# The first batch's x loads, the copies of the filter's first step and the conversion of the weights, rearranged

## The chip, the cores and the metric

The kernel runs on one core of a Trainium2 chip. The metric is the device time of one execution in microseconds (us). Five engines work side by side, each in the order of its own instructions, and wait for each other by semaphores: PE (TensorE, matmuls), DVE (VectorE), ACT (ScalarE), POOL (GpSimd), and SP (SyncE), which issues the DMAs here.

## What is computed

Two blocks in a row. The first filters x with a long convolution, the second is a gated layer on the result:

```python
h = relu(pos_emb @ w1) @ w2 * exp(-0.01 * arange(S))[:, None]      # the filter, S = 12480
y = irfft(rfft(x * v, n=2*S, axis=1) * rfft(h, n=2*S, axis=0), n=2*S, axis=1)[:, :S]
a = (x * y).reshape(4 * S, 128)                                    # 4 batches, 128 channels
t = a @ moe_w_in                                                   # 128 x 2048, float64 words
out = (t * cos(t)) @ moe_w_out                                     # 2048 x 128, float64 words
```

## The kernel before

The convolution is done by transforms of length 96 x 120, written as matmuls against tables of sines, in four steps: a first forward step (f1, matmuls of L449), a second one with the product by the filter's spectrum (f2), and two inverse steps (i1, i2). The filter and the first batch go through f1 and f2 before all else; the other three batches' transforms run beside the gated layer, which makes up most of the time. This change is wholly in the beginning, up to the end of the first batch's f1.

Program order there is laid down by hand with Python generators: a loop runs through the yields of one and calls `next` on others in between, so what is emitted at which yield fixes the order on every engine. Engines run their own instructions in that order.

- **u, the product x * v of the first batch.** `u_units` (L598) cuts it into 30 slices. For each, `u_load` loads x and v (`load_pairs`, L404), three slices ahead; `u_multiply` (L429) multiplies the two halves in place in x's tile (L431: from slice 8 on, the first half on POOL, the second on DVE), and `u_sums` (L433) writes the sum and the difference of the halves into `slots` (L441: the sum on POOL in odd slices from 9 on, all else on DVE). x and v have five buffers each, both in unused room of the big tile `slots` (class `Between`, L292), in rows of 128 elements that lie apart. So each slice takes four DMAs with runs of 512 bytes: two halves of x and two of v.
- **The filter's rows** (`filter_out`, L387, matmuls L391, copies L397 by ACT) are made from 25 to 52 us, with 52 steps of u between them.
- **f1** (`f1_units`, L625) goes through 64 channel pairs, first of the filter, then of the batch. A pair has one PSUM bank of eight, filled by four matmuls (two yields to a pair; the trace has eight rows of PE for a pair). Then it is copied out: for the filter in two copies (`f1_evict_filter`, L468 and L470), for the batch in one (`f1_evict`, L461). `taker` (L453) chooses ACT or DVE by a share: 0.8 of the filter's pairs go to ACT, which leaves DVE every fifth, and 0.75 of the batch's.
- **Conversions.** moe_w_in and moe_w_out come as float64. `convert_units` (L176) loads them as pairs of 32-bit words in 16 pieces of 256 KB (`raw`, three buffers; the first six are issued on ACT's queue, the rest by SP), makes float32 of them with integer operations, and stores them to DRAM (L190). A piece goes through all engines but PE: `float32_begin` (L142) is DVE L147 and L149, POOL L151, ACT L154 and L155, POOL L156; `float32_end` (L159) is DVE L160 and L162, POOL L166. `float32_end` of a piece is emitted just before `float32_begin` of the next.
- **The joining loop** (after L958) runs through f1's yields, numbered i. At three of four it takes a step of u, until those are done; at i = 40 it starts the conversions' first two loads, and from i = 63 on, at every ninth i, it takes a conversion step. So the first conversion stands, on every engine, right behind the last steps of u.
- **Table stores.** `store_tables` (L282) has ACT L284 and six DMAs by SP (L285 to L288), emitted before f1, that is ahead of the loads of the last nine slices of u.
- **f2** (`f2_both_units`, L653): makes its weights w with ACT L322 and DVE L324 and multiplies with L482, L485 and L135. Its first w is made when the conversions are over; its pool lies where that of the conversions was.

Of the kernel before, what the change touches and what calls it, by code (L numbers as in the profile page):

```python
# [10 lines left out]
F32 = mybir.dt.float32  # L11
# [3 lines left out]
ALU = mybir.AluOpType  # L15
# [19 lines left out]
def kernel(  # L35
# [46 lines left out]
    nc = tc.nc  # L82

    B, S, D = x.shape
# [3 lines left out]
    R = S // N2  # L88
# [8 lines left out]
    FR = 2 * (2 * N2 - 2 * N1)  # L97
    KF = N1 - 2 * (N2 - N1)
    CB = D // 2
# [5 lines left out]
    UA = 2  # L105
# [3 lines left out]
    assert G == 2 * UA and H % UA == 0 and N2 % G == 0  # L109
    LAG = 7  # L110
    ALONE = 8
    WCOL = 256

    dram = ctx.enter_context(tc.tile_pool(name="dram", bufs=1, space=DRAM))
# [24 lines left out]
        nc.tensor.transpose(dst, src, ident[0:n, 0:n])  # L139


    def float32_begin(pool, raw, factor):  # L142
        lo, hi = raw[:, :, 0], raw[:, :, 1]

        power = pool.tile([P, WCOL], U32, name="power", bufs=3)
        sig = pool.tile([P, WCOL], U32, name="sig", bufs=2)
        nc.vector.tensor_scalar(out=power[:, :], in0=hi, scalar1=20, scalar2=0x7FF,  # L147
                                op0=ALU.logical_shift_right, op1=ALU.bitwise_and)
        nc.vector.tensor_scalar(out=sig[:, :], in0=hi, scalar1=0xFFFFF, scalar2=0x100000,  # L149
                                op0=ALU.bitwise_and, op1=ALU.bitwise_or)  # L150
        nc.gpsimd.tensor_scalar(out=power[:, :], in0=power[:, :], scalar1=1023.0 - 127.0,  # L151
                                scalar2=0.0, op0=ALU.subtract, op1=ALU.max)
        high, low = sig[:, :].bitcast(F32), lo.bitcast(F32)
        nc.scalar.activation(high, sig[:, :], AF.Copy, scale=factor * 2.0 ** -20)  # L154
        nc.scalar.activation(low, lo, AF.Copy, scale=factor * 2.0 ** -52)  # L155
        nc.gpsimd.tensor_tensor(high, high, low, op=ALU.add)  # L156
        return power, hi, high

    def float32_end(power, hi, high):  # L159
        nc.vector.tensor_scalar(out=power[:, :], in0=power[:, :], scalar1=255.0,  # L160
                                scalar2=float(1 << 23), op0=ALU.min, op1=ALU.mult)
        nc.vector.scalar_tensor_tensor(  # L162
            out=power[:, :], in0=hi, scalar=0x80000000, in1=power[:, :],
            op0=ALU.bitwise_and, op1=ALU.bitwise_or)
        there = power[:, :].bitcast(F32)
        nc.gpsimd.tensor_tensor(there, high, there, op=ALU.mult)  # L166
        return there

    in_words = moe_w_in.bitcast(U32).rearrange("d (f w) -> d f w", w=2)
# [1 line left out]
    pieces = [(wind[:, c:c + WCOL], in_words[:, c:c + WCOL, :], INV_TWO_PI)  # L171
              for c in range(0, DFF, WCOL)]
# [255 lines left out]

    def u_multiply(tiles, half, engine):  # L429
        xt, vt = (t[:, half] for t in tiles)  # L430
        engine.tensor_tensor(xt, xt, vt, op=ALU.mult)  # L431

    def u_sums(u, tiles, a, takers):  # L433
# [191 lines left out]
    def f1_units(bank, u, share, evict=f1_evict):  # L625
        def mm(j, ps, i):
            if i == 0:
                ps = bank()
            f1_mm(ps, u, j, i)
            return ps  # L630

        return units(CB, F1_STEPS, lambda j: None, mm, lambda j, ps: evict(ps, j, share), 2)

    def f2_units(bank):
        with tc.tile_pool(name="there", bufs=3) as pool:
# [126 lines left out]
    def forward_units(bank, back):  # L762

        f2 = f2_units(bank)
        next(f2)
        yield from f1_units(bank, slots[0:R, :, :, :], 1.0)
        yield from f2
        next(back)
        yield from i1_units(bank)
# [114 lines left out]
    with tc.manual_schedule():  # L884
        with tc.tile_pool(name="psum", bufs=8, space=PSUM) as psum, \
                ExitStack() as first:
            def bank():
                return psum.tile([P, BANK], F32, name="ps")
# [10 lines left out]
            with tc.tile_pool(name="layers", bufs=1, side="right") as pool:  # L899
                w1_sb = pool.tile([P, P], F32, name="w1_sb")  # L900
                nc.gpsimd.memset(w1_sb[:, :], 0.0)
                pes = {0: filter_load(pool, 0)}
                for m in range(2):
                    nc.sync.dma_start(
                        w1_sb[m * FO:(m + 1) * FO, m * FO:(m + 1) * FO], w1[:, :])
                for i in range(1, NCH):
                    pes[i] = filter_load(pool, i)
                    if i == 3:
                        for m in range(2):
                            for n in range(2):  # L910
# [5 lines left out]
                first_u = u_units(0, slots[0:R, :, :, :],  # L916
                                  lambda j, half: nc.vector if half or j < ALONE else nc.gpsimd,
                                  lambda j, i: xvs[i][j % 5], 3,
                                  lambda j: (nc.gpsimd if j >= ALONE and j % 2
                                             else nc.vector, nc.vector))  # L920
# [24 lines left out]
                nc.scalar.activation(c1[:, 2, :], c1[:, 0, :], AF.Copy, scale=-1.0)  # L945
# [4 lines left out]
            for j in range(H // 2):  # L950
                filter_out(bank, aT, ftile, j, w2_sb)
                if j and j % 3 == 0:
                    last_sines.finish()
                for _ in range(2 if j % 2 or j > 15 else 1):
                    next(first_u)
            store_tables()
            keep.__exit__(None, None, None)

            backs = [inverse_units(lambda: bank(), b) for b in range(B)]

            f1 = chain(f1_units(bank, ftile[0:FR, :, :, :], 0.8, f1_evict_filter),
                       f1_units(bank, slots[0:R, :, :, :], 0.75))
            with tc.tile_pool(name="convert", bufs=1) as pool:
                convert = convert_units(pool)
                for i, _ in enumerate(f1):
                    if i % 4 < 3:
                        next(first_u, None)
                    if i == 40 or i >= 60 and i % 9 == 0:  # L970
                        if next(convert, True):
                            break
            f2 = f2_both_units(bank)
            for i, _ in enumerate(f1):
                if i == 6:
# [71 lines left out]
        for i in range(len(steps) + LAG):  # L1047
# [5 lines left out]
            if i < len(steps):  # L1053
                n, c = steps[i]
# [52 lines left out]
```

## Time and profile before

| | us |
|---|---|
| median of 3 runs | 3686.21 |
| lowest and highest run | 3684.47, 3686.36 |
| the profiled execution | 3683.9 |
| its span, first to last instruction | 3682.1 |
| PE busy in it | 3607.1 |
| DVE, POOL, ACT busy | 2814.1, 2754.7, 2228.2 |
| mean granted clock of PE | 0.997 |
| f1 of filter and batch: first L449 to first L482 | 52.44 to 153.44 |
| last product of u (POOL L441) ends | 86.75 |

All views are of the one profiled execution, and their times count from its first instruction. A row of the timeline gives start, duration, engine, line, operation and tiles, and in brackets how long the engine had stood idle before it and what released it. Matmuls of float32 are pipelined, and two rows follow each matmul instruction here. PEld is PE's weight load. The granted clock is the share of full speed that PE was allowed. The share of DMA is the mean over 16 DMA engines. A wait for several semaphores is put down to the one that came last.

### The profile page before, as it was taken

The numbers are of one execution on the slowest core, as the hardware profiler recorded it, in microseconds if no ns is written. First come the engines' busy times: TensorE is split into PE (matmuls) and PEld (weight loads), VectorE is DVE, ScalarE is ACT, GpSimd is POOL, SyncE is SP. The second block draws the span as 40 slices with busy tenths as digits, with TensorE's granted clock in tenths as the row PEclk, the third lists the DMA queues.
The fourth block names the chain that finished last, engine by engine and source line by source line (L and its number), as shares of the span: only waits on it lengthen the run. The fifth ranks groups of instructions, "written<-read, shape, count | busy, mean of one in ns | idle before, by whom it ended". The sixth has DMA issues, their size and how long they took to land.

```text
span 3682.1 us, 101741 instructions
## 1 busy us (share of the span) xinstructions
PE 3607.1 (98%) x40810; PEld 2550.9 (69%) x40810; DVE 2814.1 (76%) x5295; ACT 2228.2 (61%) x4476; POOL 2754.7 (75%) x3237
## 2 busy tenths in 40 slices
PE   8999999999999999999999999999999999999999
PEld 6777776666668776666677776766667786666666
DVE  7687886688887776688887776578887667777777
ACT  5657666655554556655555556665655446666666
POOL 7666996588874886688874887578884448878877
PEclk9999999999999999999999999999999999999999
DMA  7354540022213550022211552012220350000000
GB/s 187 111 172 126 159 145 29 18 70 70 73 47 87 171 154 29 19 70 70 72 40 36 173 167 73 13 53 70 72 69 16 89 169 22 19 23 20 19 25 14
DMA packets 226318, 281.79 MB, mean 77 GB/s; under 512 B 19168, under 2 KB 163352, under 8 KB 225720
## 3 DMA queue, kind: packets, MB, share of 16 engines
q1 hardware_dynamic: 224984, 273.71, 25.5%
q8 instruction: 324, 5.31, 0.6%
q10 hardware_dynamic: 864, 1.57, 0.1%
q14 instruction: 146, 1.20, 0.1%
HBM read 194.75 MB, written 80.46 MB: 75 GB/s over the span
## 4 chain that ended last, share of the span: by engine, by line
PE 84%; DVE 4%; ACT 1%; POOL 1%; issue 1%; DMA 0%; ACTq 0%; SPq 0%; POOLq 0%; DVEq 0%
PE ph L135 30%; PE cv L135 18%; PE accb L836 17%; PE acca L836 13%; PE cv L449 3%; PE cv L139 1%; DVE gt L811 1%; DVE gt L805 1%; PE ph L139 1%; ACT gt L804 1%; POOL ts L819 0%; ACT tile L867 0%; DVE t L504 0%; POOL ts L822 0%; POOL slots L441 0%
## 5 line engine op out<-in xcount | busy, mean ns | idle before, releaser
L804 ACT ACTIVATE gt<-ph 128x512 int32<-128x512 f32 (+1 forms) x1380 | 823.1, 596 | 1145.0 <-PE ph L135 1087.6
L805 DVE SCALAR_TENSOR_TENSOR gt<-ph,gt 128x512 f32<-128x512 f32 (+1 forms) x1380 | 949.2, 688 | 716.3 <-ACT gt L804 713.6
L819 POOL TENSOR_TENSOR ts<-gt 128x512 f32<-128x512 f32 (+2 forms) x784 | 1005.1, 1282 | 584.8 <-PE accb L836 555.3
L135 PE MATMUL ph<-at,w_in_sb 128*64 128x512 f32 (+1 forms) x5520 | 1427.1, 592 | 13.5 <-ACT tile L867 6.5
L810 ACT ACTIVATE gt<-gt 128x512 f32<-128x512 f32 (+1 forms) x1568 | 971.9, 620 | 4.1 <-DVE gt L805 3.4
L811 DVE TENSOR_TENSOR gt<-ph,gt 128x512 f32<-128x512 f32 (+1 forms) x1380 | 936.9, 679 | 0.0
L836 PE MATMUL accb<-ts,w_out_sb 128*64 128x128 f32 (+2 forms) x9408 | 650.1, 272 | 0.0
L822 POOL TENSOR_TENSOR ts<-ts,gt 128x256 f32<-128x256 f32 (+2 forms) x784 | 574.0, 732 | 61.5
L823 POOL TENSOR_TENSOR ts<-gt,ts 128x256 f32<-128x256 f32 (+2 forms) x784 | 574.0, 732 | 61.5
L836 PEld LDWEIGHTS acca<-gt,w_out_sb 128*64 128x64 f32 x6272 | 398.8, 137 | 267.7 <-issue 231.6
L836 PEld LDWEIGHTS accb<-ts,w_out_sb 128*64 128x64 f32 x9408 | 543.8, 137 | 0.0
L836 PE MATMUL acca<-gt,w_out_sb 128*64 128x128 f32 (+2 forms) x6272 | 479.2, 272 | 0.0
L836 PEld LDWEIGHTS accb<-gt,w_out_sb 128*64 128x64 f32 x3136 | 225.1, 137 | 254.4 <-issue 199.2
L135 PEld LDWEIGHTS ph<-at,w_in_sb 128*64 128x64 f32 x5520 | 353.5, 137 | 33.2 <-ACT tile L867 14.7
L505 POOL TENSOR_TENSOR slots<-slots,t 120x256 f32<-120x256 f32 x383 | 280.2, 738 | 128.6 <-DVE t L504 71.1
L135 PEld LDWEIGHTS cv<-slots,tm 96*64 96x64 f32 (+1 forms) x3840 | 243.3, 126 | 119.9 <-issue 116.0
L836 PE MATMUL accb<-gt,w_out_sb 128*64 128x128 f32 (+1 forms) x3136 | 311.1, 273 | 4.7 <-DVE ot L857 3.1
L836 PE MATMUL acca<-ts,w_out_sb 128*64 128x128 f32 (+1 forms) x3136 | 308.4, 272 | 1.4 <-POOL ts L822 1.3
L135 PE MATMUL cv<-slots,tm 96*64 96x128 f32 (+1 forms) x3840 | 274.5, 285 | 4.1 <-DVE slots L527 3.6
L135 PEld LDWEIGHTS cv<-even,slots 120*64 120x64 f32 (+1 forms) x3072 | 168.3, 125 | 60.7 <-issue 58.7
L836 PEld LDWEIGHTS acca<-ts,w_out_sb 128*64 128x64 f32 x3136 | 201.4, 137 | 2.4 <-POOL ts L822 2.2
L135 PE MATMUL cv<-slots,w 124*64 124x256 f32 (+1 forms) x1152 | 190.4, 405 | 1.9 <-ACT at L793 1.9
(137 smaller groups left out, 3742.4 us busy)
## 6 DMA issues: line engine op xcount, KB each, us to landing
h<-hd SPq DMA_DIRECT2D x144, 240.0 KB
tm<-td SPq DMA_DIRECT2D x96, 312.0 KB
xs<-in_x_dram SPq DMA_DIRECT2D x120, 208.0 KB
zd<-xs SPq DMA_DIRECT2D x119, 208.0 KB
tile<-zd SPq DMA_DIRECT2D x96, 256.0 KB
xt<-in_x_dram SPq DMA_DIRECT2D x90, 208.0 KB
vt<-in_v_dram SPq DMA_DIRECT2D x90, 208.0 KB
w<-wd SPq DMA_DIRECT2D x144, 116.2 KB
```

Of the source, the lines that this page charges most:

```text
L135: nc.tensor.matmul(dst[lo:hi], left[:, lo:hi], right, start=start, stop=stop)
L139: nc.tensor.transpose(dst, src, ident[0:n, 0:n])
L449: nc.tensor.matmul(dst[lo:hi], u[:, b, lo:hi, i], c1[0:u.shape[0], r:r + 2, :].rearrange("p r k -> p (r k)"), start=True, stop=True)
L505: (engine if r else nc.gpsimd).tensor_tensor(y[:, r], y[:, r], t[:, r], op=op)
L804: nc.scalar.activation(turns, ph[:, 0:m], AF.Identity, bias=phase)
L805: nc.vector.scalar_tensor_tensor(out=part, in0=ph[:, 0:m], scalar=phase, in1=turns, op0=ALU.add, op1=ALU.subtract)
L810: nc.scalar.activation(part, part, AF.Sin, scale=scale)
L811: nc.vector.tensor_tensor(part, ph, part, op=ALU.mult)
L819: nc.gpsimd.tensor_tensor(ts[:, 0:2, 0:half], gt[:, :, half:2 * half], gt[:, 0, 0:2 * half].rearrange("p (h n) -> p h n", h=2), op=ALU.sub ...
L822: nc.gpsimd.tensor_tensor(t[2], t[1], b11, op=ALU.add)
L823: nc.gpsimd.tensor_tensor(t[3], b21, t[2], op=ALU.subtract)
L836: nc.tensor.matmul(acc[h * CB:(h + 1) * CB, place, 0:r], w_out_sb[:, pair, weight, :], right[:, h * r:(h + 1) * r], start=(pair == 0 and i ...
```

## The change

It touches the following.

1. The first batch's x gets a pool of its own (`xpool`, five buffers), in tiles whose halves are contiguous, so `load_pairs` makes one DMA of it with runs of 1024 bytes. v stays as it was. The pool is closed when u is done, and that of the conversions is opened where it was.
2. The filter's copies: all pairs up to 36 (XV) go to ACT, the later ones by a share of 0.7; the batch's by 0.7.
3. The joining loop is cut in two: the first runs until u's steps are used up, then the tables are stored, then the second begins with the conversions' loads. Conversion steps come from i = 72 on, at every ninth i and four behind it.
4. A piece is emitted in two parts: `float32_begin` (DVE alone) and, four yields later, `float32_go_on` (POOL and ACT).
5. All raw loads are issued by SP.

```diff
-    def float32_begin(pool, raw, factor):
-        lo, hi = raw[:, :, 0], raw[:, :, 1]
+    def float32_begin(pool, raw):
+        hi = raw[:, :, 1]
...
+        return power, hi, sig
+
+    def float32_go_on(power, sig, lo, factor):
         nc.gpsimd.tensor_scalar(out=power[:, :], in0=power[:, :], scalar1=1023.0 - 127.0,
                                 scalar2=0.0, op0=ALU.subtract, op1=ALU.max)
         high, low = sig[:, :].bitcast(F32), lo.bitcast(F32)
         nc.scalar.activation(high, sig[:, :], AF.Copy, scale=factor * 2.0 ** -20)
         nc.scalar.activation(low, lo, AF.Copy, scale=factor * 2.0 ** -52)
         nc.gpsimd.tensor_tensor(high, high, low, op=ALU.add)
...
-                (nc.scalar if len(raws) < 7 else nc.sync).dma_start(
-                    raws[-1][:, :, :], pieces[len(raws) - 1][1])
+                nc.sync.dma_start(raws[-1][:, :, :], pieces[len(raws) - 1][1])
...
-                begun = float32_begin(pool, raws[i], pieces[i][2])
+                begun = float32_begin(pool, raws[i])
+                yield
+                float32_go_on(begun[0], begun[2], raws[i][:, :, 0], pieces[i][2])
             yield
...
-                xvs = [[between.tile([R, 2 * UA, D], F32).rearrange("p (h n) d -> p h n d", h=2)
-                        for _ in range(5)] for _ in range(2)]
+                vs = [between.tile([R, 2 * UA, D], F32).rearrange("p (h n) d -> p h n d", h=2)
+                      for _ in range(5)]
+                xpool = tc.tile_pool(name="x", bufs=5)
+                xs = xpool.__enter__()
+
+                def first_place(j, i):
+                    if i:
+                        return vs[j % 5]
+                    t = xs.tile([R, 2, UA * D], F32, name="xt")
+                    return t[:, :, :]
...
+            f1 = enumerate(chain(
+                f1_units(bank, ftile[0:FR, :, :, :], lambda b: 0.7 if b > XV else 1.0,
+                         f1_evict_filter),
+                f1_units(bank, slots[0:R, :, :, :], lambda b: 0.7)))
+            for i, _ in f1:
+                if i % 4 < 3 and next(first_u, None) is None:
+                    break
             store_tables()
+            xpool.__exit__(None, None, None)
             keep.__exit__(None, None, None)
...
-            f1 = chain(f1_units(bank, ftile[0:FR, :, :, :], 0.8, f1_evict_filter),
-                       f1_units(bank, slots[0:R, :, :, :], 0.75))
             with tc.tile_pool(name="convert", bufs=1) as pool:
                 convert = convert_units(pool)
-                for i, _ in enumerate(f1):
-                    if i % 4 < 3:
-                        next(first_u, None)
-                    if i == 40 or i >= 60 and i % 9 == 0:
+                next(convert)
+                for i, _ in f1:
+                    if i >= 2 * XV and i % 9 in (0, 4):
                         if next(convert, True):
                             break
```

More of the change, by code (lines that the diff above doesn't have):

```diff
@@ L111 @@
     ALONE = 8
+    XV = 36
     WCOL = 256
@@ L156, in float32_begin, with float32_end @@
         nc.gpsimd.tensor_tensor(high, high, low, op=ALU.add)
-        return power, hi, high
-    def float32_end(power, hi, high):
+    def float32_end(power, hi, sig):
         nc.vector.tensor_scalar(out=power[:, :], in0=power[:, :], scalar1=255.0,
@@ L165, in float32_end @@
         there = power[:, :].bitcast(F32)
-        nc.gpsimd.tensor_tensor(there, high, there, op=ALU.mult)
+        nc.gpsimd.tensor_tensor(there, sig[:, :].bitcast(F32), there, op=ALU.mult)
         return there
@@ L430, in u_multiply @@
         xt, vt = (t[:, half] for t in tiles)
+        if len(vt.shape) > len(xt.shape):
+            xt = xt.rearrange("p (n d) -> p n d", n=UA)
         engine.tensor_tensor(xt, xt, vt, op=ALU.mult)
@@ L630, in mm @@
             return ps
-        return units(CB, F1_STEPS, lambda j: None, mm, lambda j, ps: evict(ps, j, share), 2)
+        return units(CB, F1_STEPS, lambda j: None, mm, lambda j, ps: evict(ps, j, share(j)), 2)
     def f2_units(bank):
@@ L765, in forward_units @@
         next(f2)
-        yield from f1_units(bank, slots[0:R, :, :, :], 1.0)
+        yield from f1_units(bank, slots[0:R, :, :, :], lambda b: 1.0)
         yield from f2
@@ L913 @@
                 between = Between(slots, KE, 2 * N1)
-                xvs = [[between.tile([R, 2 * UA, D], F32).rearrange("p (h n) d -> p h n d", h=2)
-                        for _ in range(5)] for _ in range(2)]
+                vs = [between.tile([R, 2 * UA, D], F32).rearrange("p (h n) d -> p h n d", h=2)
[7 more added lines that the diff above has]
+                    return t[:, :, :]
                 first_u = u_units(0, slots[0:R, :, :, :],
                                   lambda j, half: nc.vector if half or j < ALONE else nc.gpsimd,
-                                  lambda j, i: xvs[i][j % 5], 3,
+                                  first_place, 3,
                                   lambda j: (nc.gpsimd if j >= ALONE and j % 2
@@ L955 @@
                     next(first_u)
+            backs = [inverse_units(lambda: bank(), b) for b in range(B)]
+            f1 = enumerate(chain(
[5 more added lines that the diff above has]
+                    break
             store_tables()
+            xpool.__exit__(None, None, None)
             keep.__exit__(None, None, None)
-            backs = [inverse_units(lambda: bank(), b) for b in range(B)]
-            f1 = chain(f1_units(bank, ftile[0:FR, :, :, :], 0.8, f1_evict_filter),
-                       f1_units(bank, slots[0:R, :, :, :], 0.75))
             with tc.tile_pool(name="convert", bufs=1) as pool:
                 convert = convert_units(pool)
-                for i, _ in enumerate(f1):
-                    if i % 4 < 3:
-                        next(first_u, None)
-                    if i == 40 or i >= 60 and i % 9 == 0:
+                next(convert)
+                for i, _ in f1:
+                    if i >= 2 * XV and i % 9 in (0, 4):
                         if next(convert, True):
                             break
+            f1 = (None for _ in f1)
             f2 = f2_both_units(bank)
```

## The prediction

> **What bounds the kernel now.** I read the page first: PE is busy 98% of the span and its granted clock is full nearly everywhere, so only the few stretches in which PE stands still or runs slowly can give time back. The windows view over the stretches of the first forward step (columns: us, then busy us and instructions of PE, PEld, DVE, ACT, POOL, granted clock, DMA share, GB/s) shows where they are.
> ```profile
> 62.00:84.00 22.00, 15.99 (x183) 14.42 (x179) 12.11 (x29) 7.46 (x28) 11.09 (x14) 0.88 0.78 220
> 84.00:107.00 23.00, 20.25 (x216) 16.63 (x218) 16.16 (x45) 13.89 (x55) 17.07 (x21) 0.82 0.26 87
> 107.00:138.00 31.00, 28.54 (x332) 22.18 (x328) 20.08 (x48) 18.88 (x56) 24.20 (x29) 1.00 0.34 108
> 138.00:154.00 16.00, 15.66 (x187) 13.20 (x188) 5.09 (x10) 10.87 (x27) 2.15 (x3) 1.00 0.09 26
> ```
> PE loses 6 us between 62 and 84, and the clock falls to 0.88 and 0.82. Only the last window runs freely. PE's timeline (start, us, what, idle before) shows the holes:
> ```profile
> 52.44 23.14 PE L449 MATMUL ps<-c,ftile 96*64 96x192 f32 x280 [0.55 <-ACT ftile L397]
> 76.28 0.87 PE L449 MATMUL ps<-c,ftile 96*64 96x192 f32 x8 [0.70 <-DVE slots L470]
> 81.31 1.54 PE L449 MATMUL ps<-c,ftile 96*64 96x192 f32 x8 [4.16 <-DVE slots L470]
> ...
> 138.34 15.17 PE L449 MATMUL ps<-c,slots 104*64 104x192 f32 x184 [0.53 <-ACT slots L461]
> 153.44 0.92 PE L482 MATMUL ps<-ftile,w 124*120 124x256 f32 x3
> ```
> A channel pair is 8 rows; a "slice" below is one of the 30 loads of x and v, a "piece" one of the 16 conversions. 280 rows in 23.14 us are 0.661 us a pair; 184 rows from 138.34 to 153.44 are 0.657. So 128 pairs need about 84.4 us, and the step takes 101.0 (52.44 to 153.44): 16.6 us are lost. The view of waits names the reasons in this stretch:
> ```profile
> ACT sig L154 <- DVE sig L149: 32.3, 16, 14.6
> DVE power L160 <- POOL power L151: 17.9, 16, 1.2
> POOL power L166 <- DVE power L162: 12.1, 16, 0.8
> ```
> ACT stood 14.6 us at the first conversion's L154, with the copies of PE's banks queued behind it, because DVE's L149 lay behind the last products of x and v, which ended at 86.75 (POOL L441). After that the second and third lines are a ring that paces the pieces:
> ```profile
> 111.96 0.83 DVE L160 TENSOR_SCALAR power<-power 128x256 uint32<-128x256 uint32 x1 [1.19 <-POOL power L151]
> 112.82 0.42 DVE L162 SCALAR_TENSOR_TENSOR power<-raw,power 128x256 uint32<-128x256 uint32 x1
> 113.16 0.28 DVE L147 TENSOR_SCALAR power<-raw 128x256 uint32<-128x256 uint32 x1
> ...
> 115.30 0.83 DVE L160 TENSOR_SCALAR power<-power 128x256 uint32<-128x256 uint32 x1 [1.19 <-POOL power L151]
> ```
> One piece takes 3.35 us (111.96 to 115.30): POOL's L166 cannot start before DVE's L162, nor POOL's next L151 before L166, nor DVE's next L160 before L151. PE needs only 4.5 x 0.66 = 2.97 us for the 4.5 pairs that lie between two pieces. So PE, 8 banks ahead at most, is tied to this ring until its end, and the end of the step is: start of piece 0, plus 49.6 us (86.97 to 136.59, the start of piece 15), plus what PE has left after it (136.59 to 153.44, 16.85).
>
> **The change, part by part.**
>
> *The start of piece 0.* Two things count: when the last products end, and when the first raw words are there.
>
> Products: from 41 to 56 DVE and POOL turn in a ring of their own, two slices every 3.62 us (L441 on DVE at 44.35, 47.97, 51.60, 55.22), with no wait on a DMA. Then they slip: a copy pair on DVE (0.45 + 0.25) comes in every fifth channel pair; the six table stores hold SP from 58.57 to 61.72, so the next x load issues at 61.84, some 3.3 us late; and raw loads (three of 256 KB issued on ACT's queue from 65.28 to 74.51) share the DMA engines. The waits on v's DMA on DVE and POOL, 8.8 + 9.4 us in this stretch, follow. The change takes all three away: copies of pairs 0 to 36 are ACT's, stores and raw loads come after the last x and v load. Going on at 3.62 us, DVE's sums of slice 28 start at 55.22 + 6 x 3.62 = 76.94, and POOL's last sum ends about 2.75 later (1.28 + 0.41 + handoffs + 0.97), at 79.7. The gap's memset (0.52) fits into POOL's 1.10 idle of that turn. Against 86.75: 7.0 us.
>
> Do the loads keep up? A slice is 426 KB. With 512-byte runs the trace moved 224 GB/s at a share of 0.78 (41 to 55), SP issuing without pause; I take 0.81 as the most, so some 235 GB/s, 1.81 us a slice, just the ring's pace. Single x or v loads in runs of 1024 show 273 to 293 GB/s at shares of 0.79 to 0.85 (335 to 336 us), so about 280 at 0.81: x then costs 0.76 us instead of 0.905, a slice 1.67. SP issues three DMAs a slice instead of four (0.41 each), 1.4 us instead of 1.8. I take no delay; the far bound is the rate of 224 GB/s kept, 1.90 a slice, over the 14 slices left: 1.3 us. [...] The trace's shares speak for a gain.
>
> Raw words: their pool now lies where x was, so the first load waits for the last sum (its semaphores are those of POOL's and DVE's L441 of slice 29). A new wait of about 2.8 us: the raw load issued at 89.88 moved its data from 90.85 to about 92.0, and the first pe load (issued 0.74, data until 3.3) was taken up at 4.07, so 0.7 from the last data to the taker. From below 2.6, from above 3.3 (pe's whole). Queued behind it are DVE's first copies (pair 40 on), ACT's from pair 37 on, and PE behind these. Piece 0 starts at 79.7 + 0.1 + 2.8 = 82.6 instead of 86.97.
>
> *ACT's copies.* Two per pair take 0.42 us when ACT catches up (88.14, 88.55, 88.97), under PE's 0.66, so taking all of 0 to 36 costs nothing; without that slack each pair would cost its difference. L284 moves into this slack too.
>
> *PE at the join.* ACT stops before pair 37's copy, so PE can finish pair 44: 52.44 + 45 x 0.661 = 82.2. The first copy comes after L149, L154 and L155, about 1.75 us after piece 0 starts (136.59 to 138.34 in piece 15), so PE goes on at 84.35: a hole of 2.1 us in place of 8.8. In the trace the clock fell about 1.5 us into a hole (0.84 in the us from 78) and was half until 92.3, after 5.5 us of work. If it falls, 2.75 us go; but PE then reaches pair 113 at 84.35 + 68 x 0.66 + 2.75 = 132.0, and the ring lets it start that pair only at 134.0. So this is hidden by the ring.
>
> *The parts.* Splitting begin and go-on moves POOL's and DVE's instructions past nothing of their own (their order is the same), so the ring stays 3.35. It moves ACT's L154 and L155 two pairs later and starts the pieces nine half-pairs later in PE's order, so PE is further on when the ring ends. Piece 15 starts at 82.6 + 49.6 = 132.2; ACT frees pair 41 of the second half 1.75 later, so PE starts its pair 49 there (it stood at 41 at this point before). Pair 52 waits for DVE's copy of 46 behind L162: 3.35 + 0.55 + 0.47 + handoff = 4.45 after piece 15. Then the first w (L324) waits for the last store of a converted piece, since its pool lies where the conversions were: POOL's last L166 ends 4.31 after piece 15, its store issues at 4.34 (140.93), its data is through at 142.25, 0.6 more for the receipt: 6.2; two L324 (0.6) and a copy (0.5) bring 7.45, where pair 56 would start at 7.1 otherwise. Eight pairs are left: 7.45 + 8 x 0.657 = 12.7. The receipt could take up to 1 us more (the h store issued at 156.44 is waited for until 160.49).
>
> *Sum.* Step's end: 132.2 + 12.7 = 144.9 instead of 153.44: **8.5 us**, 4.4 by the start of piece 0 and 4.1 by the later place of the pieces. Behind it the order of all engines is the same, PE bound, and shifts as a whole. The profiled execution took 3683.9 (span 3682.1) and so gives 3675.4; it lies 2.3 below the median of the runs, 3686.2, which gives 3677.7. With the bounds (products up to 1.3 later, words 0.2 earlier or 0.5 later, receipt 1 later) 3677.5 to 3680.5.
>
> **Rivals.** *The loads stay behind* (0.22): the loop of five buffers leaves 9.05 us from issue to sums, and one x load now brings both halves at once, so a slice starts only when 208 KB are there. For it: v waits of up to 3.1 us were there with 1.81 us due. Against: they began after SP's late issue. At 2.1 us a slice instead of 1.81 the start slips 4.1: 3681.8; at most 3685.
> *PE's own floor* (0.07): the ring doesn't bind, because ACT's later place lets copies through. The step would end at 52.44 + 84.4 = 136.9, 16.6 gained: 3669.6. Against: DVE's copies still lie between L149 and L160.
> *Slower* (0.05): the five buffers' loop becomes the bound with loads as slow as beside raw words, and the raw words, no longer loaded ahead, add theirs. Each us over 9.05 in the loop costs 14 / 5 = 2.8 us; no gain is left from 3.0 us over (piece 0 at 91.1), and at 5.7 over the time is 3693.7. Against: loads issued at 62.86 landed after 2.8 us (65.64).
> *It doesn't do what it says*: the changed order of instructions has one x DMA a slice and the stores behind the last load, so no chance of its own.
>
> **How the numbers follow.** Forecast 0.66, rivals 0.22, 0.07, 0.05. About 0.2% (7.4 us) can be told from no change, so faster means under 3678.8: three quarters of the forecast's share and the floor's, 0.57; slower means over 3693.6. The range of 3674.5 to 3684.5 leaves out the floor, the slower case and the edge of the second.
>
> **What would show it.** Right: POOL's last sum near 80; the first L147 2.8 us behind it, waiting on the raw words' DMA; PE's hole near 82 to 84; pieces 3.35 us apart; the first L482 near 145. Wrong: waits on v or x before 80, pieces closer or wider than 3.35, a hole between 140 and 145 longer than 1 us, or a later stage that takes the shift back.

## The result, and the profile after

The changed kernel takes 3674.12 us (median of 8 runs, 3673.44 to 3675.01), the kernel before in the same rounds 3686.18 (8 runs, 3683.81 to 3687.70): a ratio of 0.9969, 95% interval 0.9958 to 0.9979 (the two medians alone give 0.9967). It is faster by 12.1 us between the medians; between the two profiled executions by 10.1 (3683.9 and 3673.78) and between their spans by 10.9 (3682.1 and 3671.2). The prediction was 8.5 us: 3675.4 from the profiled execution, 3677.7 from the median. The measured median lies 0.4 us below the lower end of the range that was given (3674.5).

In what follows **the step** is the first forward step, **piece 0** and **piece 15** are the starts of the first and the last conversion (DVE's L148 of each; L147 in the kernel before), and **the rest** is the time from the end of the step to the end of the span. All lines lie a few later in the file: L449 became L455, L441 L447, L154 L158, L160 L163, L166 L169, L468 and L470 became L474 and L476, L461 L467.

The windows view of the changed kernel over the step (us, then busy us and instructions of PE, PEld, DVE, ACT and POOL, then granted clock, DMA share and GB/s):
```profile
62.00:84.00 22.00, 19.18 (x236) 18.81 (x231) 14.18 (x26) 12.82 (x50) 13.51 (x17) 1.00 0.67 188
84.00:107.00 23.00, 22.24 (x236) 18.14 (x238) 16.83 (x46) 14.66 (x56) 17.71 (x22) 0.85 0.34 105
130.00:146.00 16.00, 15.86 (x187) 13.57 (x188) 8.14 (x19) 11.16 (x30) 5.27 (x7) 1.00 0.11 35
```
Between 62 and 84 the trace has 236 rows of PE where it had 183, at a full clock. The clock still falls behind 84 (0.85): a hole is left. PE's timeline shows which (start, us, what, idle before and what ended it):
```profile
51.54 29.65 PE L455 MATMUL ps<-c,ftile 96*64 96x192 f32 x360 [0.55 <-POOL xt L437]
84.76 15.74 PE L455 MATMUL ps<-c,ftile 96*64 96x192 f32 x152 [3.57 <-ACT slots L476]
...
120.11 8.94 PE L455 MATMUL ps<-c,slots 104*64 104x192 f32 x104 [0.44 <-DVE slots L467]
130.14 15.17 PE L455 MATMUL ps<-c,slots 104*64 104x192 f32 x184 [1.09 <-DVE slots L467]
145.24 1.14 PE L488 MATMUL ps<-ftile,w 124*120 124x256 f32 x4
```
One hole of 3.57 us stands where three of 0.70, 4.16 and 3.90 stood. The third of these, in the timeline of the kernel before:
```profile
86.75 20.49 PE L449 MATMUL ps<-c,ftile 96*64 96x192 f32 x216 [3.90 <-DVE slots L470]
```
The step ends at 145.24 instead of 153.44: 8.2 us. The view of waits from 52 to 150 has the ring of the conversions as it was (the second and third lines of this fence are the 16 turns of before). ACT's longest wait at L158 for DVE is 1.8 us instead of 14.6, and the last line is a new wait of 7.0:
```profile
ACT sig L158 <- DVE sig L150: 18.9, 15, 1.8
DVE power L163 <- POOL power L155: 15.4, 16, 1.2
...
POOL power L169 <- DVE power L165: 12.1, 16, 0.8
...
ACT sig L158 <- DMA raw<-in_moe_w_in_dram: 7.0, 1, 7.0
```
The timeline at the join tells how long the raw words took, from the last sum of x and v to their first use:
```profile
78.70 0.97 POOL L447 TENSOR_TENSOR slots<-xt 104x256 f32<-104x256 f32 x1 [0.43 <-DVE xt L437]
...
79.70 6.43 SPq L186 DMA_DIRECT2D raw<-in_moe_w_in_dram  x4
82.97 0.29 DVE L148 TENSOR_SCALAR power<-raw 128x256 uint32<-128x256 uint32 x1 [3.88 <-DMA raw<-in_moe_w_in_dram]
83.55 0.42 ACT L158 ACTIVATE sig<-sig 128x256 f32<-128x256 uint32 x1 [6.98 <-DMA raw<-in_moe_w_in_dram]
```
The last sum ends at 79.67 (it was 86.75), the load is issued 0.03 later, and piece 0 starts at 82.97: 3.3 us of waiting for the words. At the other end, in DVE's timeline:
```profile
131.27 0.83 DVE L163 TENSOR_SCALAR power<-power 128x256 uint32<-128x256 uint32 x1 [0.72 <-POOL power L155]
...
132.48 0.29 DVE L148 TENSOR_SCALAR power<-raw 128x256 uint32<-128x256 uint32 x1
...
134.62 0.83 DVE L163 TENSOR_SCALAR power<-power 128x256 uint32<-128x256 uint32 x1 [1.19 <-POOL power L155]
...
138.97 0.59 DVE L328 SCALAR_TENSOR_TENSOR w<-even,tw_w,ps 124x120 f32<-124x120 f32 x2 [2.12 <-ACT slots L467]
```
L163 to L163 is 3.35 us, the old pace (from piece 0 to piece 15, the first turns being shorter, it is 49.5 us, where it was 49.6); piece 15 starts at 132.48, and the step ends 12.76 later.

### The profile page after: what moved, and what is told of

Its sections match the earlier page's. It is cut to its first block, busy times and chain, and to the rows that moved or that the text cites. A ratio compares the mean times of both kernels' runs of the same rounds, so it can differ in the third digit from the quotient of the medians.

```text
span 3671.2 us, 101732 instructions
## 1 busy us (share of the span) xinstructions
PE 3605.1 (98%) x40810; PEld 2553.1 (70%) x40810; DVE 2811.3 (77%) x5289; ACT 2229.7 (61%) x4482; POOL 2757.7 (75%) x3237
## 4 chain that ended last, share of the span: by engine, by line
PE 85%; DVE 4%; ACT 1%; POOL 1%; issue 1%; DMA 0%; ACTq 0%; DVEq 0%; POOLq 0%; SPq 0%
PE ph L136 30%; PE cv L136 18%; PE accb L842 17%; PE acca L842 13%; PE cv L455 3%; PE cv L140 1%; DVE gt L817 1%; DVE gt L811 1%; PE ph L140 1%; ACT gt L810 1%; POOL ts L825 0%; DVE t L510 0%; ACT tile L873 0%; DVE slots L508 0%; POOL ts L828 0%
```

## The experiments

Theory at the start: the step's end is piece 0 plus a fixed stretch that the ring sets, and piece 0 comes earlier because the last products do. Rivals: one part alone makes the gain (the copies' shares, the split, the longer runs), or the gain lies behind the step. All eleven kernels were timed in rounds beside the kernel before, whose medians in the three groups were 3686.39 (24 runs), 3686.36 (7) and 3685.68 (24); the first two groups ran on one chip, the third on another. Each place in the step comes from one profile. Times in us:

| kernel | last sum ends | piece 0 | step ends | piece 0 to end | median (range, runs) | ratio, 95% interval |
|---|---|---|---|---|---|---|
| before | 86.75 | 86.97 | 153.44 | 66.47 | 3686.18 (3683.8–3687.7, 8) | |
| before again | 88.51 | 88.74 | 155.20 | 66.46 | 3685.56 (3684.2–3689.3, 10) | 1.0000 [0.9991, 1.0010] |
| changed | 79.67 | 82.97 | 145.24 | 62.27 | 3674.12 (3673.4–3675.0, 8) | 0.9969 [0.9958, 0.9979] |
| changed again | 79.73 | 82.77 | 145.04 | 62.27 | 3673.67 (3673.0–3674.7, 5) | 0.9966 [0.9953, 0.9979] |
| old shares | 81.08 | 84.03 | 145.86 | 61.83 | 3676.89 (3674.3–3678.9, 10) | 0.9975 [0.9966, 0.9985] |
| one part | 79.76 | 82.77 | 145.88 | 63.11 | 3675.26 (3673.8–3676.2, 7) | 0.9970 [0.9959, 0.9982] |
| from step 63 | 80.21 | 83.17 | 148.80 | 65.63 | 3677.89 (3675.3–3679.6, 10) | 0.9977 [0.9968, 0.9987] |
| runs of 512 | 79.92 | 83.22 | 145.52 | 62.30 | 3675.59 (3674.0–3676.3, 6) | 0.9969 [0.9957, 0.9981] |
| stores first | 83.66 | 86.63 | 148.88 | 62.25 | 3676.52 (3674.1–3679.0, 8) | 0.9973 [0.9962, 0.9984] |
| stores and raw words amid | 84.84 | 84.88 | 147.14 | 62.26 | 3677.42 (3674.7–3679.3, 10) | 0.9978 [0.9969, 0.9987] |
| raw words early | 80.18 | 80.24 | 142.50 | 62.26 | 3673.04 (3671.8–3674.1, 5) | 0.9962 [0.9948, 0.9977] |
| no ring | 80.38 | 83.38 | 139.28 | 55.90 | 3669.62 (3668.5–3671.4, 4) | 0.9954 [0.9937, 0.9972] |
| both | 79.77 | 81.28 | 137.18 | 55.90 | 3665.82 (3664.7–3666.8, 4) | 0.9942 [0.9927, 0.9958] |

The fifth column is the main finding. It is 62.25 to 62.30 in all six profiles whose pieces and shares of the copies are those of the change, whatever the start of piece 0 (80.24 to 86.63) and whatever the holes; 66.46 and 66.47 in the two of before. Nor does the clock count there: behind the join it was low for 6.8 us in the changed kernel, for 3.4 in its second profile and not at all with the raw words early, and the stretch was 62.27, 62.27 and 62.26.

The last sum is less firm: in the seven profiles of kernels that are equal up to it, or differ only in what is loaded behind the stores, it ends between 79.67 and 80.38, and in the two of before 1.76 us apart.

### Old shares of the copies
```diff
-                f1_units(bank, ftile[0:FR, :, :, :], lambda b: 0.7 if b > XV else 1.0,
+                f1_units(bank, ftile[0:FR, :, :, :], lambda b: 0.8,
                          f1_evict_filter),
-                f1_units(bank, slots[0:R, :, :, :], lambda b: 0.7)))
+                f1_units(bank, slots[0:R, :, :, :], lambda b: 0.75)))
```


> The changed kernel with the old shares (0.8 of all filter pairs and 0.75 of the batch's to ACT), so DVE has a pair of copies (0.45 + 0.25 us) at every fifth channel pair while it still makes the products. Theory (DVE's copies slow the products): each pair of copies adds some 0.65 us to the products' 3.62 us ring, seven of them fall between 52 and 78 us, so POOL's last sum ends at about 84 instead of 79.7, the first conversion starts at about 87 instead of 83.0, f1 ends at about 149 to 150 instead of 145.2, and the time is about 3678 to 3679. Rival (the copies fit into DVE's waits of 0.62 us a turn, and the late table stores and raw loads were all): last sum at 80, f1's end at 145, 3674.

The theory asked too much: the last sum moved by 1.4 us, not by 4. DVE's copies are a small part of the products' delay. What they cost PE itself shows in its timeline in this kernel:
```profile
62.64 17.51 PE L455 MATMUL ps<-c,ftile 96*64 96x192 f32 x192 [1.81 <-DVE slots L476]
...
124.61 21.32 PE L455 MATMUL ps<-c,slots 104*64 104x192 f32 x256 [0.52 <-DVE slots L467]
```
DVE's copy (L476 at 62.25) lay behind a sum of x and v (L447), and PE stood 1.81 us. But in the second half, where the share is 0.75, PE runs freely from 124.61, in the changed kernel only from 130.14; the end is 0.6 us later, though piece 0 is 1.06 later (61.83 between them against 62.27). Both shares were changed together, so that the second one is the reason is not shown apart. The median, 2.8 above the changed kernel's, is more than that, which stays open below.

### Pieces in one part, and pieces from step 63
```diff
                 begun = float32_begin(pool, raws[i])
-                yield
                 float32_go_on(begun[0], begun[2], raws[i][:, :, 0], pieces[i][2])
...
-                    if i >= 2 * XV and i % 9 in (0, 4):
+                    if i >= 2 * XV and i % 9 == 0:
```
and, as a kernel of its own, in two parts but from half-pair 63 on:
```diff
-                    if i >= 2 * XV and i % 9 in (0, 4):
+                    if i >= 63 and i % 9 in (0, 4):
```


> The changed kernel with each piece emitted in one part again (POOL's and ACT's instructions right behind DVE's, every ninth yield from 72 on). Theory (the ring of DVE and POOL sets the pace, DVE's copies behind L150 and L165 set what PE has left): piece 0 still at 83.0, pieces 3.35 us apart, f1's end at 145.2 to 146.2, since ACT's copies now stand two pairs more behind L158 and cost at most 0.8 us once at the end; 3674 to 3675.5. Rival (the two parts are what freed ACT): waits of ACT of 1.2 us or more at each piece show up on PE, f1's end at 148 or later, 3677.

> The changed kernel with the conversion steps from yield 63 on instead of 72, so that they stand 4.5 channel pairs earlier in PE's order. Theory (PE is tied to the ring until its end, so what is left after the last piece counts): piece 0 at 83.0 and the last at 132.5 as before, PE's hole begins 3 us earlier, f1 ends 4.5 x 0.657 = 3.0 us later, at 148.2; 3677. Rival (PE isn't tied to the ring): f1's end unchanged at 145.2 within 0.5, 3674.

Both theories held. The split changes the step's end by 0.64 us (145.88 against 145.24), the place of the pieces by 3.56 (148.80). PE's last start after a hole, in the timeline of the kernel with one part and then of the one from step 63, with the hole at the join ahead of it:
```profile
84.84 15.55 PE L454 MATMUL ps<-c,ftile 96*64 96x192 f32 x168 [4.13 <-ACT slots L475]
...
134.03 11.92 PE L454 MATMUL ps<-c,slots 104*64 104x192 f32 x144 [0.56 <-ACT slots L466]
```
```profile
133.69 15.17 PE L455 MATMUL ps<-c,slots 104*64 104x192 f32 x184 [1.09 <-DVE slots L467]
```
From step 63 PE has the same 184 rows left as in the changed kernel (15.17 us of them), and starts them at 133.69 instead of 130.14. The pieces come nine half-pairs earlier in PE's order, which is one piece; so the copy by DVE that sets PE free lies behind piece 15 (132.69) there, in the changed kernel behind the piece ahead of it (129.13). That is one turn of the ring, 3.35 us, and piece 0 is 0.20 later.

### x in runs of 512 bytes
```diff
-                    return t[:, :, :]
+                    return t.rearrange("p h (n d) -> p h n d", n=UA)
```
With this shape each slice of x is loaded by two DMAs again, into the same pool.

> The changed kernel with x in its own pool, but loaded by two DMAs a slice in runs of 512 bytes, as v is. Theory (the runs aren't what brings the products forward; order of stores, raw loads and copies is): last sum at 79.7 to 81, f1's end at 145.2 to 146.5, 3674 to 3675.5. Rival (the longer runs are needed for the loads to keep up with 3.62 us for two slices): waits on the DMAs of x and v of several us in all, last sum at 83 or later, f1's end at 148.5 or later, 3677.5 or more.

The last sum ends at 79.92 against 79.67 and the step 0.28 later: the long runs, and the one DMA less a slice, bring nothing that counts once stores and raw words are out of the way. There were waits for x and v here that the changed kernel does not have (six of products, L437, between 57 and 74 us, 0.26 to 1.13 long), but the ring made up for them. From 41 to 55 us the loads moved 234 GB/s at a share of 0.76 here; with the long runs it was 209 at 0.75 and, in the second profile, 241 at 0.91. So the long runs moved no more for the same share, and the gain in rate that the prediction read from shares (280 GB/s against 235) was not there. But the ring set the pace in both kernels, so no run measures the most that the loads could move.

### Stores first, and the raw words amid the loads
```diff
+            store_tables()
             for i, _ in f1:
+                if i == 40:
+                    early = list(first_raws(between))
                 if i % 4 < 3 and next(first_u, None) is None:
                     break
-            store_tables()
```
The two lines with `first_raws` are in the second kernel only (the lines that read these tiles in their other shape are left out here): it loads the first three raw tiles, on ACT's queue, into free room of the large tile, so that they wait for no pool.

> The changed kernel with the six table stores back ahead of the first forward step, so that they hold SP's queue among the last loads of x and v, all else as changed. Theory (the late x load behind the stores was the larger part of the products' delay, since the old shares of the copies alone brought the last sum only from 79.7 to 81.1): a load issues some 3 us late, the buffers' slack takes a part of it, the last sum ends at 82 to 83, piece 0 starts at 85 to 86.3, the step ends at 147.5 to 148.5, the time is about 3677. Rival (the five buffers hide the stores): last sum at 80, the end at 145.3, 3674.

> As the kernel before it in this call (the stores ahead of the step) and with the first three raw loads also back among the last loads of x and v: issued on ACT's queue at half pair 40, into free room of the large tile, so that nothing waits for a place. Copies' shares and the two-part pieces stay as changed. Theory (the raw words' 768 KB lie on the DMA engines when x and v need them): the last sum ends another 2 to 3 us later than with the stores alone, at 84.5 to 86, piece 0 starts right there with no wait for raw words, the step ends at 147 to 148, the time is about 3676.5. Rival (the loads share without harm): last sum where the stores alone put it, piece 0 right there at 80 to 83, the step's end at 142.5 to 145, the time 3672 to 3674.

The first theory held in kind, with sizes at or above its upper ends: the stores alone put the last sum back by 4.0 us (83.66 where 82 to 83 was expected, and the step's end at 148.88 where 147.5 to 148.5 was). SP's timeline in the first kernel, and then a wait that followed, from DVE's:
```profile
55.56 0.45 SPq L289 DMA_DIRECT2D csd<-slots  x1
56.11 1.06 SPq L290 DMA_DIRECT2D csd<-slots  x1
58.39 0.32 SPq L289 DMA_DIRECT2D csd<-slots  x1
...
60.70 0.50 SPq L412 DMA_DIRECT2D xt<-in_x_dram  x1
```
```profile
69.26 0.63 DVE L437 TENSOR_TENSOR xt<-xt,slots 104x256 f32<-104x256 f32 x1 [2.90 <-DMA slots<-in_v_dram]
```
Six stores held SP's queue for 5 us, waits for their sources among it, and the waits for v came back. The raw words add 1.2 us (84.84), less than the 2 to 3 expected, and nothing waits for them: piece 0 follows the sum by 0.04. So the second kernel's step ends 1.7 us ahead of the first kernel's. The medians do not show that order (3677.42 and 3676.52), but the ranges overlap almost wholly. Stores 4.0, raw words 1.2 and copies 1.4 make 6.6 of the 7.1 us by which the last sum moved. That they add up is not shown: the copies were put back alone, the raw words on top of the stores, and 1.2 and 1.4 are only about twice the 0.7 by which equal kernels differ.

### Raw words early, no ring, both
```diff
             store_tables()
+            early = list(first_raws(between))
...
-            made = float32_end(*begun) if begun else None
-            begun = None
-            load(i + 3)
+            last, begun = begun, None
             if i < len(pieces):
                 begun = float32_begin(pool, raws[i])
                 yield
                 float32_go_on(begun[0], begun[2], raws[i][:, :, 0], pieces[i][2])
+            made = float32_end(*last) if last else None
+            load(i + 3)
```
The first hunk (loads on SP's queue, again without the lines that read the tiles) is the kernel with raw words early, the second, with three buffers of `sig` instead of two, the one without the ring; the third kernel has both.

> The changed kernel with the first three raw loads in room of the big tile that is free until the batch's f1 copies come (where the old x buffers lay), issued right behind the table stores, so they no longer wait for the last product. Theory (the wait for the raw words is the new cost at the join, 3.3 us from the last sum at 79.7 to piece 0 at 83.0, and the ring carries it to f1's end): piece 0 at 79.8, PE's hole at 81 to 85 gone or under 0.5 us and the clock full there, pieces 3.35 us apart, f1's end at 142 instead of 145.2, 3671. Rival (the ring isn't tied to its start, PE's lost time at the join is hidden anyway): hole gone, but f1's end at 145, 3674.

> The changed kernel with the ring of a piece opened: the end of a piece is emitted behind the second part of the next (a third buffer for sig), so POOL's L155 no longer waits for the product of the piece before. Theory (the ring of 3.35 us is what ties PE): pieces come at POOL's own 2.64 us until they have caught up, then at PE's 2.97; the small waits of PE after 100 us go; the hole of 3.6 us at the join and the half clock behind it (3.2 us) stay and are now the whole loss: f1's end at 51.5 + 84.4 + 6.8 = 142.7, 3671.6. Rival (something else sets the 3.35 us, as DVE's waits for banks or the stores of pieces): pieces still 3.3 us apart, f1's end at 145, 3674.

> Both edits together: the first three raw words loaded early and the ring of a piece opened. Theory: no hole at the join, no ring behind it; PE is the bound of f1, which ends at 51.5 + 84.4 plus 1 to 2 us, 137 to 138; the time 3666 to 3668 if the stages behind only shift. Rival (the stage after f1 takes it back: the first w waits for the last store of a piece, or the clock falls in another place): f1's end at 138, but the time at 3670 or above.

The first two theories held for the step in kind, the third but for the hole at the join. With the words there in time, piece 0 starts 0.06 after the last sum and the fixed stretch follows (80.24 + 62.26 = 142.50). The time is 2 us above the expected 3671: in its profile the rest took 3528.5 us, 2.5 more than in the first profile of the changed kernel. DVE's first conversion in that kernel no longer waits for a DMA:
```profile
80.24 0.29 DVE L155 TENSOR_SCALAR power<-slots 128x256 uint32<-128x256 uint32 x1 [0.65 <-PE ps L470]
```
With the end of a piece behind the second part of the next one, the ring is gone: pieces come 2.74 us apart on average (83.38 to 124.50) and PE, in its timeline, has no hole after the join:
```profile
53.24 29.64 PE L455 MATMUL ps<-c,ftile 96*64 96x192 f32 x360 [0.55 <-ACT ftile L401]
85.17 12.57 PE L455 MATMUL ps<-c,ftile 96*64 96x192 f32 x152 [2.29 <-ACT slots L476]
97.58 41.77 PE L455 MATMUL ps<-c,slots 104*64 104x192 f32 x512
```
The 512 rows of the second half take 41.77 us, 0.653 a pair: PE is the bound. The hole was 2.29 us here, not the expected 3.6, and the clock did not fall behind it (1.00 from 84 to 100), so the end, 139.28, is better than the expected 142.7.

Both edits together end the step at 137.18, within the expected 137 to 138, and give 3665.82 us, ratio 0.9942 (0.9927 to 0.9958): faster than either kernel of the case. The expected "no hole at the join" did not come. DVE's first conversion waited for the words again, 1.51 us from the last sum (79.77), and PE stood 1.04:
```profile
81.28 0.29 DVE L155 TENSOR_SCALAR power<-slots 128x256 uint32<-128x256 uint32 x1 [2.09 <-DMA slots<-in_moe_w_in_dram]
```
```profile
83.08 12.57 PE L470 MATMUL ps<-c,ftile 96*64 96x192 f32 x152 [1.04 <-ACT slots L491]
```
SP issued the early loads at 77.80 here, behind a table store that took it 1.42 us, and at 76.29 in the kernel above. So loads behind the stores can come too late: the words were in time in the one profile and not in the other.

### Both kernels once more


> The changed kernel itself, unaltered, for a second profiled execution. Question: the shift against the kernel before grew by 1.7 us in one step near 560 us, where the same hole of 2.35 us of PE is followed by a half clock in the profile of before and by a full clock in the profile of after. Theory (which holes are followed by a fall of the clock differs from execution to execution, so the 1.7 us are no property of the change): the step's end stays at 145.2 within 0.3, but the list of clock falls differs, at 245 or at 560. Rival (the place of the hole, 8.8 us earlier, decides): no fall at 560 again, a fall at 245 again, the same shifts. The time 3673 to 3676 in either case.

> The kernel before itself, unaltered, for a second profiled execution beside the one above. Theory (falls differ by execution): the first step's end at 153.4 within 0.4, and the falls behind 256 and 570 not both as in the first profile. Rival (the place decides): falls at 256 to 260 and at 570 to 574 again, and the same total. The time 3684 to 3688 in either case.

These two ask why the gain was larger than the step's 8.2 us. Segments of the four profiles, cut at the step's end, at two copies of the middle stage on ACT (`tile<-ph`) and at the end of the span:

| us | before | before again | changed | changed again |
|---|---|---|---|---|
| to the step's end | 153.44 | 155.20 | 145.24 | 145.04 |
| to the first copy | 395.97 | 394.95 | 395.36 | 394.82 |
| to the second copy | 37.80 | 36.11 | 36.12 | 37.80 |
| to the end of the span | 3094.9 | 3095.0 | 3094.5 | 3095.0 |
| span | 3682.1 | 3681.3 | 3671.2 | 3672.7 |

In the third row each kernel once takes 37.8 and once 36.1. All four have the same hole of 2.34 or 2.35 us of PE there; the windows view over the five us behind it, in the order of the table:
```profile
569.00:574.00 5.00, 4.86 (x39) 3.91 (x39) 0.39 (x1) 1.01 (x2) 4.76 (x6) 0.66 0.44 134
```
```profile
569.00:574.00 5.00, 4.46 (x48) 3.68 (x50) 0.93 (x3) 1.49 (x3) 4.84 (x6) 1.00 0.48 111
```
```profile
560.00:565.00 5.00, 4.86 (x54) 3.99 (x55) 1.29 (x2) 1.49 (x3) 4.77 (x6) 1.00 0.46 123
```
```profile
559.00:564.00 5.00, 4.74 (x32) 3.92 (x34) 0.00 (x0) 0.15 (x1) 4.76 (x7) 0.66 0.44 118
```
The granted clock is 0.66, 1.00, 1.00 and 0.66: the same hole cost 1.7 us more in one execution than in another, in either kernel. The theory held there: those 1.7 us are no property of the change. The other fall, behind a hole of 2.95 to 2.98 us that ends near 245 (near 256 in the kernel before), came in all four, as the rivals said of that place; it lasted about 3.4 us in three of them and 6.8 in the first of the changed kernel. In all thirteen profiles of the table the rest took between 3525.1 and 3529.0 us, the four here being spread over most of that.

The other thing that the repetition shows is the first row. The changed kernel's step ends at the same place (145.24 and 145.04), that of before does not (153.44 and 155.20), because its last sum moves. POOL's timeline in the second profile of before:
```profile
87.54 0.97 POOL L441 TENSOR_TENSOR slots<-slots 104x256 f32<-104x256 f32 x1 [0.42 <-DVE slots L431]
```
Its end, 88.51, is 1.76 later than the 86.75 on which the forecast was built; the expectation, 153.4 again, missed this. So the step gave 8.2 us in one pair of profiles and 10.2 in the other.

## Why the prediction was right, point by point

**The sum.** 8.5 us were forecast for the step, 8.2 and 10.2 came. Its end was put at 144.9: 145.24 and 145.04. The mechanism of the step was right, and its terms stand as follows. That 8.5 lies so near to 8.2 is in part luck, since the place that it starts from, the last sum of before, moved by 1.76 us between two executions. The time gained 12.1 us between the medians, 3.6 more than forecast, and that part is not in any term.

**Products, last sum at 79.7:** 79.67 and 79.73. The ring of 3.62 us per two slices ran to the end, as predicted. The one wait on v that the profile names between 40 and 80, POOL's 1.10 at 42.38, is as long as POOL's wait for DVE in every other turn, and the second profile names none. The three reasons were right too; by weight they are the stores (4.0), DVE's copies (1.4) and the raw words (1.2). The share of 0.81 that was taken as the most was the author's assumption: in the changed kernel it was 0.90 in each us from 60 to 63 (249 to 272 GB/s). The far bound of 1.3 us for slower loads was not needed, but not because the long runs are faster: with runs of 512 bytes the loads were waited for at times, and it cost 0.25 us at the last sum, which is within the scatter of equal kernels.

**Raw words, 2.8 us (2.6 to 3.3):** 3.30 and 3.04, in the other profiles 2.95 to 3.30 wherever the pool had to come free first. This term was sized too low; the upper end was the better row. The row that it went by (89.88) was one load alone, while here three loads of 256 KB were issued one behind the other within 1.3 us and the DMA engines were full (a share of 1.04 in the us from 82); that this is the reason is not shown.

**PE's hole, 82.2 to 84.35:** it reached from 81.19 to 84.76 in one profile and was 2.46 us in the other, and the clock fell behind both. As predicted, the ring hid that: 62.27 us from piece 0 to the end in both.

**The ring, 3.35 us a piece, piece 15 at 132.2:** 3.35 us; 132.48, later by what the raw words took more.

**The end, 12.7 after piece 15:** 12.76, but not by the steps given. The prediction let PE start its last stretch after ACT's L158 of piece 15 and then wait twice, for DVE's copy of pair 46 and for the first w behind the last store. In the trace PE's last wait was for DVE's copies ahead of piece 15 (130.14), and from there it ran 15.1 us without a hole. The first w started at 138.97, 6.5 after piece 15 where 6.2 was forecast. The profile puts its wait down to a copy on ACT, but that had ended 0.28 us before, and the last store had been issued at 136.81. In the eight profiles in which such a copy is named, the first w comes 2.0 to 2.3 us after the issue of the last store and 0.05 to 0.40 after the copy; so the wait for the store, as forecast, is the likelier reading. The 0.6 us that the forecast put behind the last data, for a receipt, no run shows as such: in the changed kernel the DMA engines were idle from 138.50, and the first w came 2.16 us after the issue of the last store, where 1.9 was forecast. It delayed nobody. The size of the end was right; the waits of PE in it were not there.

**4.4 us by the start of piece 0, 4.1 by the later place of the pieces:** 4.0 (86.97 to 82.97) and 4.2 (66.47 to 62.27). The place makes 3.4 of the second (65.63 in the kernel from step 63), the split 0.8 (63.11 in one part). The new shares of the copies, which the prediction priced at nothing here, seem to take 0.4 back (61.83 with the old ones), so the parts do not quite add up.

**"Shifts as a whole":** this is the step that failed in its size. The order behind the step is the same, but the clock is not: the rest took 3528.7, 3526.1, 3526.0 and 3527.7 us in the four profiles, with no order by kernel. Between the first two profiles it added 2.7 us to the gain (8.2 became 10.9), between the second two it took 1.6 away (10.2 became 8.6). And the time was carried over to the median from one execution of before whose step was 1.8 us shorter than in the second.

**What stays open.** The profiled executions differ by 10.1 and 9.5 us in time, the medians by 12. The profiled executions of before lie 2.3 and 1.3 us below the medians of its runs, those of the changed kernel 0.3 below and 1.1 above. Kernels with stores, raw words or copies amid the loads, that of before among them, scatter more (3.9 to 5.0 us over 8 to 10 runs) than the changed one (1.6 and 1.7 over 8 and 5), but the one from step 63, which has none of these, scatters by 4.3. That the unprofiled runs of before mostly have a later last sum would fit; no trace of them shows it.

**The rivals.** Loads that stay behind: no, nothing was lost to a wait on x or v. PE's own floor: not in the changed kernel, and 137.18 when the ring and a part of the wait for raw words were taken away, where 136.9 was given. Slower by the loop of five buffers: no.

## What to carry to other kernels

Where a loop over two engines (here DVE and POOL) paces a stage, look for its start and its length before anything else: the end followed the start within 0.05 us, while holes and clock falls ahead of it cost nothing. Stores that no one needs yet belong behind the last load of their queue; here six small ones cost 4 us, three loads of 256 KB amid the others 1.2. A chain that waits on the other engine twice a turn may be broken by emitting the end of one piece behind the beginning of the next, with one more buffer; here that was worth more than any part of this change (6 us of the step).

## What the runs showed of the hardware

A hole of PE of 2.34 or 2.35 us was followed by half a clock in two of four executions (a granted clock of 0.66 over the five us behind it, 1.00 in the other two), one of 2.95 to 2.98 in all four (low for about 3.4 us in three of them, for 6.8 in one). At the join one of 2.29 was not (1.00 from 84 to 100), one of 2.46 was (0.50 from 86 to 88). In the kernel with the old shares the clock was low from 64 to 68 (0.54 and 0.61 in the two halves), 1.4 us after the end of the hole of 1.81 us. So holes of 1.8 to 3.0 us were already followed by half a clock, the longest of these in each of the four executions. What decides it for the shorter ones no run here shows.

The load of raw words of 256 KB, the first of three in a row, took 2.95 to 3.30 us from the end of the last reader of their place to their first use, in eight profiles.
